# Value and key sums turned in one held-back transfer, and a unit's query sum turned by TensorE

## The chip, the cores and the metric

The kernel runs on one core of one Trainium2 chip. The metric is device time in microseconds (us) from one launch, the median over several runs. The engines of a core work in parallel, each on its own list of instructions in the order in which the program has them: TensorE (PE in the profile; its weight loads are PEld), VectorE (DVE), ScalarE (ACT), GpSimd (POOL) and SyncE (SP), which here does nothing but issue DMA transfers. An instruction that waits holds up everything behind it on its engine.

## The reference, cut to what matters

```python
def _A_ref(x, wqkv, wo):                       # x: 1 x 2048 x 576, 32 heads of 18
    q, k, v = split_heads(x @ wqkv)
    p = softmax(q @ k.T * 18 ** -0.5)
    return merge_heads(p @ v) @ wo

def _fwd_reference(...):
    g = sigmoid((x * gate_w).sum(-1, keepdims=True))
    return g * _A_ref(x, wqkv, wo) + (1 - g) * _B_ref(x, ...)

_out, _vjp = jax.vjp(_f, A_x, A_wqkv, A_wo, ...)
return (_out, *_vjp(grad_out))
```

The kernel returns the output and the gradients of all inputs. The attention part A takes the middle of the run. Its backward part needs, for every head, the gradients of q, k and v over all 2048 positions; they go to a DRAM tensor `dqkv_d`, from which later stages work out the gradients of x and wqkv. Part B, a long convolution, is worked on by GpSimd beside the attention and by all engines after it.

## The kernel before

The heads are taken in 8 groups of 4. A group's positions are cut into 4 blocks of 512, and one *unit* is one group with one block of queries: 32 units. A unit runs over 16 tiles of 128 keys, in 32 *steps* (the loop variable `G` counts steps over all units; the list of each engine is written out by hand in the order of the loop). The forward part of a unit runs 39 steps ahead of its backward part. Below, *s* counts the backward steps from the start of a group's last unit: 0 to 31 is that unit, and 32 to 63 is the first unit of the next group.

In each step TensorE makes scores in two layouts and the products with the gradient of the output (tiles `ps_P`). ScalarE takes two exponentials of them (`PT`, `eb`), VectorE two products (`ds`). The sums over them are collected in bursts, in slots that repeat every 8 steps: value sums (`accV`), query sums (`accQ`), a slot in which TensorE turns (transposes) something, key sums (`accK`), and another turn slot. With kq the block of 512 keys, the bursts of a unit end at steps 8 kq + 8 (values), 8 kq + 10 (queries) and 8 kq + 13 (keys).

The key sums need `ds` transposed. A tile of `ds` holds 4 heads by 512 queries. SyncE issues a transposing DMA for it (`dsT<-ds`, L1473) that turns 3 of the 4 heads for most tiles; the fourth is turned by TensorE in a turn slot, two tiles at a time (`turn`, L1105 on; `by_pe` says how many of a pair p of tiles TensorE turns: 2, but 0 for pair 5, which loses its slot to another job, and 1 for pair 6, which shares it). VectorE copies what TensorE turned out of PSUM. The two DMAs of pair p are issued in steps 4 p + 1 and 4 p + 3 of the unit, and the burst that needs them starts 6 steps after the second. There are 3 buffers for a pair.

The gradients come out with heads along partitions, and `dqkv_d` wants positions there, so each finished sum of 128 x 512 is turned as well (`store_grad`, L1080). Two steps after the burst's end SyncE issues a transposing DMA into a tile `gT` (3 buffers). Four steps later GpSimd copies the 18 useful columns of each head out of it into `dtk` (one buffer), and stores that by a DMA of its own. A query sum (`gb`) is ready at the end of every unit, and value and key sums (`dvacc`, `dkacc`, 4 buffers each, rounded to bfloat16 in place) at the end of every group: 32 + 32 + 32 of these transfers. In the steps s the value sums go at 10, 18, 26 and 34, the query sum at 36, and the key sums at 15, 23, 31 and 39.

SyncE's list holds, besides these, the loads of the next group's operands (`KaT`, `QaT`, `VaT`, and transposing `Ktok`, `Vtok`, `Qtok`) and the turn of part of `PT` (`PTt`, L1126). GpSimd's list holds the convolution's powers (`Eo`, `et`), which a budget deals out over the steps (`e_emit`; each pack of a gradient counts 1.4 us in it), and in step 2 of a forward unit two small products (`dOa`, `prod`, L1061 and L1063) for which VectorE waits one step later.

Of the kernel before, what the change touches and what calls it, by code (L numbers as in the profile page):

```python
# [11 lines left out]
BF = mybir.dt.bfloat16  # L12
# [5 lines left out]
P = 128  # L18


def build(tc, aps, dbg_aps=None, stages=("s1", "attn", "post", "s4", "final")):
    nc = tc.nc
# [16 lines left out]
    S, D = x2.shape  # L39
    H = 32  # L40
    DH = D // H
    F = 3 * D
    NT = S // P
    HP = 32
# [14 lines left out]
    NG = H // 4  # L59

    with ExitStack() as gctx:
# [20 lines left out]
        dqkv_d = dram.tile([P, NT, F], BF, name="dqkv_d")  # L82
# [497 lines left out]
        Q = {}  # L580
# [370 lines left out]
        if "attn" in stages:  # L951
            KB = 512
            NQ = S // KB
            TPQ = KB // P
# [4 lines left out]
            with ExitStack() as ctx:  # L959
# [67 lines left out]
                UN = {}  # L1027
                DKV = {}
# [47 lines left out]
                def in_place(t_):  # L1076

                    return t_.bitcast(BF)[:, 0:KB]

                def store_grad(gb, g, which, t0):  # L1080
                    c0 = which * D + g * 4 * DH
                    gT = work.tile([P, TPQ, 4, HP], BF, tag="gT", bufs=3, name="gT")
                    nc.sync.dma_start_transpose(out=gT.rearrange("p t a b -> p t (a b)"), in_=gb)

                    def pack():
                        dtk = work.tile([P, TPQ, 4, DH], BF, tag="dtk", bufs=1, name="dtk")
                        nc.gpsimd.tensor_copy(dtk, gT[:, :, :, 0:DH])
                        nc.gpsimd.dma_start(dqkv_d[:, t0:t0 + TPQ, c0:c0 + 4 * DH], dtk.rearrange("p t a b -> p t (a b)"))
                    packs.append((now[0] + 4, pack))

                packs, now = [], [0]

# [6 lines left out]

                def by_pe(u, p):  # L1100

                    return 2 if u == units[-1] else {NPF: 0, NPF + 1: 1}.get(p, 2)

                def turn(tiles, outs):

                    pt_ = apsp.tile([P, len(tiles), TPQ, P], BF, tag="accB", name="turn_p")
                    for x, t_ in enumerate(tiles):
                        for qb in range(TPQ):
                            nc.tensor.transpose(pt_[:, x, qb, :], t_[:, qb * P:(qb + 1) * P], ident_bf)  # L1109

                    def ev():
                        x = 0
                        for n, o_ in outs:
                            (nc.scalar.copy if NTOT <= now[0] < NTOT + OFF else nc.vector.tensor_copy)(o_(), pt_[:, x:x + n])  # L1114
                            x += n
# [12 lines left out]
                def turn_mid(i):  # L1128

                    U = UN[units[-1]]  # L1130
                    pt_ = s_pair("turn").rearrange("p a b -> p (a b)").bitcast(BF)[:, 0:2 * KB].rearrange("p (t b) -> p t b", b=P)
                    for x in range(2):
                        for qb in range(TPQ):
                            nc.tensor.transpose(pt_[:, x * TPQ + qb, :], U["ds"][i][:, 1 + x, qb * P:(qb + 1) * P], ident_bf)
                    d_ = U["dsT", i // 2][:, i % 2, TPQ:3 * TPQ, :]
                    return lambda: (nc.scalar.copy if now[0] < NTOT + OFF else nc.vector.tensor_copy)(d_, pt_)

                def do_tile(U):
                    U["dOaT"] = work.tile([P, TPQ, P], BF, tag="dOaT", name="dOaT")
# [10 lines left out]
                def at(n, f):  # L1150
                    todo.setdefault(n, []).append(f)
# [11 lines left out]
                def dv_half(g, b, kq, h, acc):  # L1163
                    U = UN[(g, b)]

                    def stored(ii):
                        for j in range(4):
                            w = KT if j < 2 else KB
                            mm(acc[HP * j:HP * (j + 1), 0:w], lhsT=U["dOa"][:, ii, j, :], rhs=U["eb"].pop((kq, ii, j)),
                               start=(ii == 0), stop=(ii == 3), tile_position=(0, HP * j))  # L1170

                    def turned(ii):
                        for j in range(2):
                            mm(acc[HP * j:HP * (j + 1), KT:KB], lhsT=U["dOa"][:, ii, j, :], rhs=U["PTt", kq][:, j * TPQ + ii, :],
                               start=False, stop=False, tile_position=(0, HP * j))
                    stored(2 * h)
                    turned(2 * h)
                    turned(2 * h + 1)
                    if h == 0:
                        stored(1)  # L1180
                    else:
                        late.append(lambda: stored(3))

                    def ev():
                        if b == 0:
                            DKV[("v", g, kq)] = work.tile([P, KB], F32, tag="dvacc", bufs=4, name="dvacc")
                            nc.vector.tensor_copy(DKV[("v", g, kq)], acc)
                            return
                        a_ = o_ = DKV[("v", g, kq)]
                        if b == NQ - 1:  # L1190
                            o_ = DKV[("v", g, kq)] = in_place(a_)
                        nc.vector.tensor_tensor(o_, a_, acc, op=A.add)  # L1192
                    return ev

# [18 lines left out]
                def dk_half(g, b, kq, h, acc):  # L1213
                    U = UN[(g, b)]
                    o_ = acc[:, 2 * h * P:2 * (h + 1) * P]
                    for qb in range(TPQ):
                        for j in range(4):
                            mm(o_[HP * j:HP * (j + 1), :].rearrange("p (a b) -> p a b", b=P), lhsT=grp_t[g]["Qtok", b][:, qb, HP * j:HP * (j + 1)],
                               rhs=U["dsT", 2 * kq + h][:, :, j * TPQ + qb, :], start=(qb == 0), stop=(qb == TPQ - 1), tile_position=(0, HP * j))

                    def ev():
                        if b == 0:
                            DKV[("k", g, kq)] = work.tile([P, KB], F32, tag="dkacc", bufs=4, name="dkacc")
                            nc.vector.tensor_copy(DKV[("k", g, kq)], acc)
                            return
                        a_ = o_ = DKV[("k", g, kq)]
                        if b == NQ - 1:
                            o_ = DKV[("k", g, kq)] = in_place(a_)
                        nc.vector.tensor_tensor(o_, a_, acc, op=A.add)
                    return ev  # L1230

# [110 lines left out]
                for G in range(NTOT + OFF + 24):  # L1342
# [37 lines left out]
                    if ("f1", G) in todo:  # L1380
                        acc = apsp.tile([P, KB], F32, tag="accO", name="accF")
                        evs.append(todo.pop(("f1", G))[0](acc))
                        e_done[0] += 1.4
                    elif G == NST + 5:
                        evs.append(turn(*do_tile(UN[units[0]])))
                    elif 0 <= m_ < NTOT // 8:
                        u_, kq = divmod(m_, NQ)
                        g, b = units[u_]
                        if slot in SLOTS:
                            nm, burst, h = SLOTS[slot]  # L1390
                            if h == 0:
                                acc = accB("acc" + nm)
                                fill(acc, NFILL[nm])
                                burst(g, b, kq, 0, acc)
                            else:
                                evs.append(burst(g, b, kq, 1, acc))
                                if nm == "Q" and kq == NQ - 1:
                                    at(("pre", G + 2), lambda g=g, b=b: store_grad(UN[(g, b)].pop("dqa"), g, 0, b * TPQ))
                                elif nm in "KV" and b == NQ - 1:
                                    at(("pre", G + 2), lambda g=g, kq=kq, nm=nm: store_grad(DKV.pop((nm.lower(), g, kq)), g, 1 + "KV".index(nm), kq * TPQ))  # L1400
# [541 lines left out]
```

## Time and profile before

| | us |
|---|---|
| median of 3 runs | 2599.77 |
| lowest and highest run | 2592.21, 2615.22 |
| the profiled execution, its own time | 2605.51 |
| its span from the first to the last instruction | 2603.5 |
| TensorE busy | 2263.8 (87%) |
| VectorE busy | 2279.8 (88%) |
| ScalarE busy | 2260.6 (87%) |
| GpSimd busy | 1838.9 (71%) |
| mean granted TensorE clock | 0.965 |

The page's sixth part lists the DMA issues by line: `dsT<-ds` 512 times, `PTt<-PT` 128 times, and `gT<-gb`, `gT<-dvacc` and `gT<-dkacc` 32 times each, all by SyncE as transposing transfers, and `dqkv_d<-dtk` 96 times by GpSimd. In the page's waits a line reads "engine line waited for: us in total, times, longest". In the table of windows each row is a stretch of time with the busy time of each engine, the number of its instructions, the granted TensorE clock (1.00 is full speed) and the mean busy share of the 16 DMA engines, which can be over 1 because packets overlap. In a timeline a row is the start, the time taken, the engine and line, and in brackets the idle time before it and what ended that. For SyncE the time taken is that of issuing, not that of the transfer.

### The profile page before, as it was taken

How to read it: one execution, taken by the hardware profiler on the slowest of the kernel's cores; microseconds unless marked ns; L12 is line 12 of the kernel's file. 1: busy time of each engine (PE TensorE's matmuls, PEld its weight loads, DVE VectorE, ACT ScalarE, POOL GpSimd, SP SyncE). 2: the span in 40 equal slices, each digit the busy share in tenths (PEclk: the TensorE clock that was granted, in tenths of full speed). 3: DMA queues.
4: the chain of work that ended last, by engine and by line, in shares of the span. 5: the costliest groups of instructions: out<-in, count | busy, mean ns of one | idle time of the engine just before them, and what ended most of it. 6: DMA issues, size and time to landing. Idle time of an engine off the chain costs nothing. (4 is left out here: it accounts for less than half of the span.)

```text
span 2603.5 us, 72402 instructions
## 1 busy us (share of the span) xinstructions
PE 2263.8 (87%) x28467; PEld 1163.1 (45%) x28467; DVE 2279.8 (88%) x4091; ACT 2260.6 (87%) x2760; POOL 1838.9 (71%) x2859
## 2 busy tenths in 40 slices
PE   7998888888888788788888888888889799999989
PEld 4433333333333333333333333333334699998656
DVE  4849898999899899889989998999997699999964
ACT  5579999999999999999999999999997599999211
POOL 0389988898889888979888988898951155555331
PEclk9979998999999999999989999999999799999999
DMA  7749999999999999999999999999989789997995
GB/s 236 198 119 184 170 191 194 193 189 198 189 192 188 198 200 179 196 195 183 187 203 178 188 194 203 182 191 199 175 170 180 199 240 264 267 261 238 276 251 133
DMA packets 1273708, 518.92 MB, mean 199 GB/s; under 512 B 1188513, under 2 KB 1226002, under 8 KB 1271062
## 3 DMA queue, kind: packets, MB, share of 16 engines
q1 hardware_dynamic: 1225446, 368.05, 74.8%
q0 software_dynamic: 45904, 140.73, 20.2%
q10 hardware_dynamic: 2016, 5.51, 0.7%
q8 instruction: 223, 3.65, 0.6%
q14 instruction: 119, 0.97, 0.1%
HBM read 149.42 MB, written 96.94 MB: 95 GB/s over the span
## 5 line engine op out<-in xcount | busy, mean ns | idle before, releaser
L1463 DVE TENSOR_TENSOR ds<-ps_P,PT 128x512 bf16<-128x512 f32 x2048 | 1321.8, 685 | 71.8 <-PE ps_P L30 61.2
L1453 ACT ACTIVATE PT<-ps_P 128x1024 bf16<-128x1024 f32 x1024 | 1111.3, 1086 | 18.9 <-PE ps_P L30 17.3
L1458 ACT ACTIVATE eb<-ps_P 128x896 bf16<-128x896 f32 x1024 | 995.6, 973 | 55.1 <-PE ps_P L30 54.4
L30 PE MATMUL ps_P<-dOaT,VaT_g 32*128 32x512 bf16 x2048 | 792.5, 390 | 7.1 <-DVE ds L1463 6.2
L30 PE MATMUL ps_P<-QaT_g,KaT_g 32*128 32x512 bf16 x2048 | 410.3, 390 | 198.7 <-ACT PT L1453 169.4
L507 POOL TENSOR_TENSOR et<-eG,eT 128x448 f32<-128x448 f32 x576 | 542.8, 963 | 10.8
L30 PE MATMUL ps_P<-KaT_g,QaT_g 32*128 32x384 bf16 (+1 forms) x2048 | 407.0, 365 | 4.4 <-ACT eb L1458 0.8
L30 PEld LDWEIGHTS <-KaT_g 32*128 32x128 bf16 x2048 | 161.0, 92 | 488.7 <-issue 464.6
L507 POOL TENSOR_TENSOR Eo<-et,et 128x448 bf16<-128x448 f32 x288 | 327.2, 1136 | 21.0
L30 PEld LDWEIGHTS <-QaT_g 32*128 32x128 bf16 x2048 | 107.0, 91 | 245.1 <-issue 209.1
L30 PE MATMUL accO<-PT,Vtok_g 128*32 128x512 bf16 x2048 | 215.4, 398 | 1.0 <-DVE Ob L1059 0.5
L30 PE MATMUL accV<-eb,dOa 128*32 128x384 bf16 (+1 forms) x2048 | 189.4, 375 | 8.1 <-DVE dsT L1114 7.3
L30 PE MATMUL accK<-dsT,Qtok_g 128*32 128x256 bf16 x4096 | 163.1, 280 | 31.0 <-DMA dsT<-ds 28.8
L30 PEld LDWEIGHTS <-VaT_g 32*128 32x128 bf16 x2048 | 184.3, 91 | 3.7 <-issue 2.1
L30 PE MATMUL accQ<-ds,Ktok_g 128*32 128x512 bf16 x2048 | 161.2, 392 | 23.6 <-DVE dvacc L1192 18.0
L1114 DVE COPY dsT<-turn_p 128x1024 bf16<-128x1024 bf16 (+1 forms) x216 | 139.7, 647 | 2.4 <-PE turn_p L1109 2.4
L1109 PE MATMUL turn_p<-ident_bf,ds 128*128 128x128 bf16 x1676 | 136.4, 224 | 2.0 <-DVE gb L1210 0.8
L30 PEld LDWEIGHTS <-dOa 128*32 128x32 bf16 x3072 | 79.4, 96 | 131.4 <-issue 96.4
L30 PEld LDWEIGHTS <-Qtok_g 128*32 128x32 bf16 x4096 | 88.1, 97 | 99.6 <-issue 79.2
L673 ACT COPY E1e<-etp 128x1024 bf16<-128x1024 bf16 x132 | 125.3, 1064 | 1.8 <-PE etp L672 1.8
L507 POOL TENSOR_TENSOR et<-eT 128x32 f32<-128x32 f32 (+3 forms) x288 | 116.3, 424 | 11.1
L1109 PEld LDWEIGHTS <-ds 128*128 128x128 bf16 x1676 | 99.2, 100 | 48.2 <-issue 48.0
(301 smaller groups left out, 3771.3 us busy)
## 6 DMA issues: line engine op xcount, KB each, us to landing
E_d<-Eo POOLq DMA_DIRECT2D x144, 256.0 KB, 3.6
E1n<-E_d POOLq DMA_DIRECT2D x30, 1024.0 KB, 6.9
T0w<-Kp_d SPq DMA_DIRECT2D x18, 1024.0 KB
xs<-xb_d POOLq DMA_DIRECT2D x28, 512.0 KB, 10.1
dsT<-ds SPq DMA_TRANSPOSE x512
dqkv_d<-dtk POOLq DMA_DIRECT2D x96, 72.0 KB, 4.5
Md_d<-mst SPq DMA_DIRECT2D x18, 288.0 KB
skw<-Md_d SPq DMA_DIRECT2D x72, 64.0 KB
```

What stands on the lines that cost most here:

```text
L30: return nc.tensor.matmul(out, lhsT=lhsT, rhs=rhs, start=start, stop=stop, **kw)
L507: nc.gpsimd.tensor_tensor(out, a, b, op=op)
L673: copy(E_[:, 4 * q:4 * q + 4], pt_)
L1109: nc.tensor.transpose(pt_[:, x, qb, :], t_[:, qb * P:(qb + 1) * P], ident_bf)
L1114: (nc.scalar.copy if NTOT <= now[0] < NTOT + OFF else nc.vector.tensor_copy)(o_(), pt_[:, x:x + n])
L1453: nc.scalar.activation(U["PT"][i, j // 2], ps, ACT.Exp)
L1458: nc.scalar.activation(e, ps.rearrange("p x q -> p (x q)")[:, KB - KT:2 * KB], ACT.Exp)
L1463: nc.vector.tensor_tensor(U["ds"][i][:, j, :], ps, U["PT"][i, j // 2][:, j % 2, :], op=A.mult)
```

## The change

- A group's value sum and key sum of the same block of keys are now put side by side in one buffer of `dvacc`: the key sum's last addition writes into its second half. One transposing DMA of twice the width turns both. It is issued 11, 19, 18 and 18 steps after the burst of the key sum for blocks 0 to 3 (2 steps in the last group), so at s = 24, 40, 47 and 55. GpSimd's two packs follow 4 and 6 steps later.
- A query sum is no longer turned by a DMA, but for the last two units. TensorE turns it in the next unit's slot of pair 1 (s = 43 at a group's end), together with one of the two tiles of that pair; VectorE copies it out of PSUM straight into `dtk`, and GpSimd only stores it, two steps later.
- For that, `by_pe` gives 1 for pair 1: the first tile of pair 1 is now turned whole (4 heads) by its DMA.
- `gT` has one buffer of double width in place of three, `dtk` has two in place of one.

```diff
-                def store_grad(gb, g, which, t0):
-                    gT = work.tile([P, TPQ, 4, HP], BF, tag="gT", bufs=3, name="gT")
+                def store_grad(gb, g, whichs, t0):
+                    n = len(whichs)
+                    gT = work.tile([P, 2 * TPQ, 4, HP], BF, tag="gT", bufs=1, name="gT")[:, 0:n * TPQ]
                     nc.sync.dma_start_transpose(out=gT.rearrange("p t a b -> p t (a b)"), in_=gb)
...
-                        dtk = work.tile([P, TPQ, 4, DH], BF, tag="dtk", bufs=1, name="dtk")
+                        dtk = work.tile([P, TPQ, 4, DH], BF, tag="dtk", bufs=2, name="dtk")
...
-                    packs.append((now[0] + 4, pack))
+                    for x in range(n):
+                        packs.append((now[0] + 4 + 2 * x, lambda x=x: pack(x)))
...
-                    return 2 if u == units[-1] else {NPF: 0, NPF + 1: 1}.get(p, 2)
+                    return 2 if u == units[-1] else {1: 1, NPF: 0, NPF + 1: 1}.get(p, 2)
...
+                def gb_tile():
+                    U, g, b = gq.pop(0)
+                    gb = U.pop("dqa")
+                    dtk = work.tile([P, TPQ, 4, DH], BF, tag="dtk", bufs=2, name="dtk")
+                    packs.append((now[0] + 2, lambda: nc.gpsimd.dma_start(dqkv_d[...], dtk.rearrange("p t a b -> p t (a b)"))))
+                    return [gb], [(0, lambda: dtk)]
...
+                            DKV.pop(("k", g, kq))
+                            o_ = DKV[("v", g, kq)].bitcast(BF)[:, KB:2 * KB]
...
-                                elif nm in "KV" and b == NQ - 1:
-                                    at(("pre", G + 2), lambda g=g, kq=kq, nm=nm: store_grad(...))
+                                elif nm == "K" and b == NQ - 1:
+                                    at(("pre", G + (2 if g == NG - 1 else (11, 19, 18, 18)[kq])), lambda g=g, kq=kq: store_grad(...))
...
+                            if p == 1 and gq:
+                                t2, o2 = gb_tile()
+                                t_, o_ = t2 + t_, o2 + o_
```

SyncE's list at the end of the third group, s = 31 to 39 before. The sizes are partitions, blocks of 128 and columns; a `dsT` of 12 blocks is 3 heads.

```order
L1083 DMA_TRANSPOSE gT_15843<-dkacc_12303 128x4x128
L1473 DMA_TRANSPOSE dsT_15798<-ds_15831 128x12x128
L1126 DMA_TRANSPOSE PTt_15915<-PT_14693 128x8x128
L1473 DMA_TRANSPOSE dsT_15943<-ds_15907 128x12x128
L1083 DMA_TRANSPOSE gT_15951<-dvacc_12416 128x4x128
L1473 DMA_TRANSPOSE dsT_15943<-ds_15973 128x12x128
L1019 DMA_TRANSPOSE Ktok_g_16014<-QKV_d_72 128x8x128
L1083 DMA_TRANSPOSE gT_16016<-gb_15975 128x4x128
L1473 DMA_TRANSPOSE dsT_16090<-ds_16051 128x12x128
L1009 DMA VaT_g_16104<-QKV_d_72 128x512
L1083 DMA_TRANSPOSE gT_16138<-dkacc_12599 128x4x128
L1473 DMA_TRANSPOSE dsT_16090<-ds_16127 128x12x128
```

SyncE's list after the change from the `Ktok` load on, s = 35 to 49.

```order
L1019 DMA_TRANSPOSE Ktok_g_15967<-QKV_d_72 128x8x128
L1495 DMA_TRANSPOSE dsT_16049<-ds_16002 128x16x128
L1009 DMA VaT_g_16058<-QKV_d_72 128x512
L1495 DMA_TRANSPOSE dsT_16049<-ds_16081 128x12x128
L1083 DMA_TRANSPOSE gT_16134<-dvacc_11777 128x8x128
L1130 DMA_TRANSPOSE PTt_16176<-PT_14940 128x8x128
L1495 DMA_TRANSPOSE dsT_16204<-ds_16164 128x12x128
L1009 DMA QaT_g_16239<-QKV_d_72 128x512
L1495 DMA_TRANSPOSE dsT_16204<-ds_16230 128x12x128
L1495 DMA_TRANSPOSE dsT_16349<-ds_16306 128x12x128
L1083 DMA_TRANSPOSE gT_16385<-dvacc_12077 128x8x128
L1495 DMA_TRANSPOSE dsT_16349<-ds_16376 128x12x128
```

The four single turns of s = 31 to 39 are gone, the first tile of pair 1 has 16 blocks, and the double turns of blocks 1 and 2 stand at s = 40 and 47; the second stands ahead of the second tile of pair 3.

GpSimd's list after the change at the same group's end, where the values of block 1, the query sum and the keys of block 1 are stored; `dtk_16247` is what VectorE wrote in step 43.

```order
L507 TENSOR_TENSOR et1_16271<-eG_1237,eT_1236 128x448
L1088 COPY dtk_16311<-gT_16134 128x288
L1089 DMA dqkv_d_75<-dtk_16311 128x4x72
L1149 DMA dqkv_d_75<-dtk_16247 128x4x72
L1088 COPY dtk_16382<-gT_16134 128x288
L1089 DMA dqkv_d_75<-dtk_16382 128x4x72
L507 TENSOR_TENSOR Eo_16132<-et0_16237,et1_16271 128x4x112
```

Before, nothing of the gradients stood here on GpSimd's list. With two `dtk` buffers in turn, the keys' copy takes the buffer that the query sum's store, right ahead of it, still reads; and the double turn at s = 47 takes the `gT` tile that this copy reads.

VectorE's list after the change in the slot of pair 1, where it has two copies; before there was one, of 128 x 2 x 512, for the two tiles of the pair.

```order
L1485 TENSOR_TENSOR ds_16230<-ps_P2_16245,PT_14825 128x512
L1118 COPY dtk_16247<-turn_p_16248 128x288
L1118 COPY dsT_16049<-turn_p_16248 128x512
L1485 TENSOR_TENSOR ds_16230<-ps_P2_16260,PT_14825 128x512
L1485 TENSOR_TENSOR ds_16306<-ps_P2_16276,PT_14865 128x512
```

The query sum's copy stands ahead of the tile's.

More of the change, by code (lines that the diff above doesn't have):

```diff
@@ L1113, in ev @@
                         for n, o_ in outs:
-                            (nc.scalar.copy if NTOT <= now[0] < NTOT + OFF else nc.vector.tensor_copy)(o_(), pt_[:, x:x + n])
-                            x += n
+                            src_ = pt_[:, x:x + n] if n else pt_[:, x].rearrange("p t (a b) -> p t a b", b=HP)[:, :, :, 0:DH]
+                            (nc.scalar.copy if NTOT <= now[0] < NTOT + OFF else nc.vector.tensor_copy)(o_(), src_)
+                            x += max(n, 1)
                     return ev
@@ L1190, in ev @@
                         if b == NQ - 1:
-                            o_ = DKV[("v", g, kq)] = in_place(a_)
+                            o_ = in_place(a_)
                         nc.vector.tensor_tensor(o_, a_, acc, op=A.add)
```

20 lines of the change are left out of this document (13 added, 7 removed).

## The prediction

> **What bounds the kernel now.** I read the waits of the attention stage first (235 to 1950 us), then a table of windows, then SyncE's timeline where a window was bad. Waits, in columns engine, line, waited for, total, times, longest:
>
> ```profile
> ACT eb L1458 <- PE ps_P L30: 44.3, 38, 4.6
> ...
> POOL dtk L1087 <- DMA dqkv_d<-dtk: 29.9, 19, 3.2
> ...
> PE accK L30 <- DMA dsT<-ds: 22.9, 13, 4.2
> ...
> DVE dOa L1069 <- POOL prod L1063: 7.3, 6, 2.1
> ```
>
> ScalarE hardly ever waits: 44.3 us here, in few long waits for TensorE, which in turn waits for the transposed `ds`. The windows say where. The first two rows and the first sum are of the 7 stretches at the ends of groups 1 to 7 (48 steps each), the last two are of the stretches between them.
>
> ```profile
> 822.00:912.00 90.00, 73.02 (x919) 29.40 (x916) 79.32 (x132) 83.99 (x98) 77.20 (x129) 0.96 1.10 198
> 1051.00:1144.00 93.00, 76.14 (x922) 30.11 (x921) 79.91 (x132) 84.90 (x98) 77.72 (x126) 0.93 1.05 198
> ...
> sum 623.00, PE 520.50 PEld 204.59 DVE 555.34 ACT 587.88 POOL 526.08; mean PE 74.36 PEld 29.23 DVE 79.33 ACT 83.98 POOL 75.15
> ...
> 683.00:822.00 139.00, 119.35 (x1511) 47.41 (x1508) 132.12 (x222) 138.92 (x161) 125.79 (x207) 1.00 1.03 187
> ...
> sum 1076.00, PE 920.69 PEld 363.55 DVE 1013.39 ACT 1065.85 POOL 946.29; mean PE 115.09 PEld 45.44 DVE 126.67 ACT 133.23 POOL 118.29
> ```
>
> Between the ends ScalarE is busy 138.92 of 139 us: it sets the pace there, 161 exponentials or 80 steps in 139 us, so **1.74 us a step**. At the ends it idles 623.0 - 587.9 = **35.1 us** in all, about 5 a group; between them 1076.0 - 1065.9 = 10.2 us. Only the 35.1 us stand near what the change moves. A third set of windows shows why a wait costs more than itself:
>
> ```profile
> 1340.00:1346.00 6.00, 4.97 (x59) 1.75 (x57) 5.62 (x11) 6.00 (x8) 3.84 (x9) 1.00 1.30 200
> ...
> 1349.00:1352.00 3.00, 0.90 (x16) 0.45 (x16) 0.00 (x0) 0.18 (x1) 1.15 (x4) 0.75 1.20 215
> 1352.00:1355.00 3.00, 3.00 (x27) 1.32 (x24) 2.21 (x4) 1.94 (x2) 2.83 (x8) 0.50 1.08 195
> ...
> 1361.00:1364.00 3.00, 3.00 (x26) 0.46 (x18) 1.92 (x3) 2.34 (x3) 2.63 (x4) 0.50 1.03 197
> ```
>
> After a wait of some 3 us the clock is at 0.50 for 12 us, TensorE is busy throughout and ScalarE starves: between 0.7 and 1.1 us lost in each 3 us, so about 3 us behind a wait of 3. A wait under a microsecond has no such tail to show.
>
> The cause, in SyncE's timeline at the end of group 3 (start, time to issue), with TensorE's wait last:
>
> ```profile
> 878.85 1.38 SPq L1019 DMA_TRANSPOSE Ktok_g<-QKV_d  x1
> 880.32 1.61 SPq L1083 DMA_TRANSPOSE gT<-gb  x1
> 882.02 1.67 SPq L1473 DMA_TRANSPOSE dsT<-ds  x1
> 883.74 0.57 SPq L1009 DMA_DIRECT2D VaT_g<-QKV_d  x1
> 884.42 1.20 SPq L1083 DMA_TRANSPOSE gT<-dkacc  x1
> 885.70 1.44 SPq L1473 DMA_TRANSPOSE dsT<-ds  x1
> 887.25 1.63 SPq L1126 DMA_TRANSPOSE PTt<-PT  x1
> ...
> 891.40 1.05 PE L30 MATMUL accK<-dsT,Qtok_g 128*32 128x256 bf16 x16 [3.36 <-DMA dsT<-ds]
> ```
>
> SyncE issues without a gap. It is late: VectorE finished this query sum from 869.42 on, and its turn goes out 10.9 us later; in the first unit of all the same two stand 3.9 us apart.
>
> ```profile
> 869.42 0.68 DVE L1210 SCALAR_TENSOR_TENSOR gb<-accQ,dqa 128x512 bf16<-128x512 f32 x1
> ...
> L1210 DVE SCALAR_TENSOR_TENSOR gb<-accQ,dqa x32: 680/681/692, 239.7 to 2018.6; 128x512 bf16<-128x512 f32 x32
> ...
> 243.62 1.19 SPq L1083 DMA_TRANSPOSE gT<-gb  x1
> ```
>
> So SyncE is about 7 us behind, and the tile issued at 885.70 was wanted at 888.0 (891.40 less the wait of 3.36) and came at 891.4. Its flight, issue included, was 5.7 us.
>
> **The change, part by part.** *Single turns go from the crowded place.* Each costs SyncE 1.2 to 1.25 us:
>
> ```profile
> L1083 SPq DMA_TRANSPOSE gT<-dvacc x32: 1194/1246/2259, 369.3 to 2026.6; - x32
> L1083 SPq DMA_TRANSPOSE gT<-dkacc x32: 1191/1195/2352, 376.6 to 2032.2; - x32
> ```
>
> Between s = 10 and 39, nine of them (8 and the query's) make 9 x 1.23 = 11 us; one double turn at s = 24 comes in, at about 1.3 us, what the equally wide `PTt` takes in the tail rows below. SyncE gains 9.8 us over these 30 steps of 52 us and was 7 behind at their end, so the backlog should be gone at s = 39, and with it the waits of pair 1. The most this can bring is the 35.1 us. The bytes stay: every query sum that a DMA no longer turns is replaced by a fourth head of `ds` in pair 1, two tiles' time earlier than its need.
>
> *Double turn at s = 47, with one `gT` buffer.* It waits until GpSimd has copied the keys of block 1, and SyncE holds everything behind it. No row shows this wait; it is built from these (the last is the landing of GpSimd's stores of `dtk`):
>
> ```profile
> 1288.36 1.27 SPq L1083 DMA_TRANSPOSE gT<-dvacc  x1
> ...
> 1298.58 0.43 POOL L1087 COPY dtk<-gT 128x288 bf16<-128x288 bf16 x1
> 1299.31 0.80 POOL L1088 DMA_DIRECT2D dqkv_d<-dtk  x1 [0.29 <-POOL dtk L1087]
> ...
> DMA to landing us min/median/max: 2.5/4.5/7.9
> ```
>
> From a turn's issue to GpSimd's copy, four steps later on the list, it is 10.2 us, of which GpSimd's own lateness is about 1.5. So after an issue at step 40 the values' copy starts at 10.2 us, the query's store 1.5 later (0.43 + 0.29 + 0.80), and the keys' copy must await its landing, 4.5 us: 16.2, done at 16.6. Step 47 starts at 7 x 1.74 = 12.2 us. SyncE is held 4.5 to 5.4 us (the second if the turn at 40 is as late as the 0.9 us in this row). The tile behind it, the second of pair 3, then goes at 5 + 1.3, lands 4.6 (a wait in group 2, below) to 6.2 us later, at 10.9 to 12.5 us; the burst that needs it starts 6 steps on, at about 10.4 + 0.6 = 11.0. A wait of 0 to 1.5 us, too short for the slow clock: I take 1 us a group, **7 us**. The ends: nothing, if GpSimd runs early; up to 10 us a group (a rival, below). At s = 55 GpSimd has two more steps of which one is lost to its lateness; a hold of 1 to 2 us there is inside pair 5's slack.
>
> ```profile
> 626.89 2.46 SPq L1473 DMA_TRANSPOSE dsT<-ds  x1
> ...
> 631.46 1.04 PE L30 MATMUL accK<-dsT,Qtok_g 128*32 128x256 bf16 x16 [1.65 <-DMA dsT<-ds]
> ```
>
> *VectorE.* One copy of 1024 columns becomes one of 512 and one of 288:
>
> ```profile
> L1114 DVE COPY dsT<-turn_p 128x1024 bf16<-128x1024 bf16 x186 | 127.1, 683 | 2.4 <-PE turn_p L1109 2.4
> ...
> L1114 DVE COPY dsT<-turn_p 128x512 bf16<-128x512 bf16 x30 | 12.6, 419 | 0.0
> ...
> L1059 DVE TENSOR_TENSOR Ob<-accF,rl 128x288 bf16<-128x288 f32 x32 | 14.6, 457 | 1.1
> ```
>
> By the line through the first two, 288 columns take 155 + 288 x 0.52 = 303 ns: 39 ns more, 30 times, **1.2 us**; with 457 ns as upper end 5.8 us; nothing as lower end, since VectorE has 7 us to spare in the 139 us above. *TensorE* turns 8 blocks in that slot as before: nothing. *GpSimd* loses 30 copies of 0.43 us and most waits for its one `dtk` buffer (29.9 us above), and gains the 3.7 us wait a group just built. It is not the bound, but when it is late VectorE waits (`dOa <- prod`, 7.3 us above), and the 10.2 us between the ends hang on that. I cost it at nothing, between -6 and +8 us. *The end of attention*: SyncE has three singles fewer ahead of the last double turn (3.7 us), which lands later by its second half, and GpSimd's two copies after it hold `pidx_i`, for which ScalarE waited:
>
> ```profile
> 2009.08 1.26 SPq L1126 DMA_TRANSPOSE PTt<-PT  x1
> ...
> 2024.24 1.19 SPq L1083 DMA_TRANSPOSE gT<-dkacc  x1
> ...
> 2029.49 0.43 POOL L1087 COPY dtk<-gT 128x288 bf16<-128x288 bf16 x1 [5.53 <-DMA gT<-dkacc]
> ...
> ACT RX L604 <- DVE l1col L1506: 16.6, 1, 16.6
> ```
>
> I take **-1 us**, between -4 and +3.
>
> **The sum**, against the profiled execution's own 2605.5 us (span 2603.5, 2 us around it): -35.1 + 7 + 1.2 + 0 - 1 = -28, so 2577.5. That execution is 5.7 us above the median of the runs, 2599.8, and from that the same sum gives 2572. How much of the 5.7 is such waits is not shown; I put 2574.
>
> **The rivals.** *The same bytes (no change).* If the waits come from the load on the DMA engines and not from the number of issues, merging helps little: the share of the DMA engines is 1.10 and 1.05 in the bad windows, but also 1.03 in a clean one, and 1.30 in one with ScalarE fully busy. For it speaks that issues stretch there (2.46 us above for a usual 1.4) and that the `Ktok` and `VaT` loads stay. Half of the 35.1 would remain: -17.5 + 7 + 0.2 = -10, 2590, up to 2600. The Trainium skill, in "DMA: Bandwidth & Descriptors", section "Issuing engines are not separate DMA queues", says that all transfers run on the same 16 engines and that the time to initiate one is usually small relative to it; by that page the merging itself would be worth little and this rival's 2590 to 2600 would be the forecast. Here the issue is 1.44 of 5.7 us and SyncE has no gap, so the trace does not bear it out at the groups' ends.
>
> *SyncE held too long (slower).* The hold at s = 47 is 5 us by a median landing. With the longest, 7.9 us, and GpSimd 3 us later from its own wait, it is 11 to 12, the tile lands at 17 to 19.5 us, TensorE waits 6 to 8 and the slow clock adds 3: 10 us, 7 times, 70, so 2600 - 35 + 70 = 2635. It decides from a hold of about 8 to 9 us, where wait and tail give back the 5 us a group.
>
> *All of it goes (faster).* No hold matters, and GpSimd's shorter list clears the 10.2 us as well: 2600 - 35 - 10 + 1 = 2556.
>
> **Chances.** Forecast, 2564 to 2583: 0.48. All goes: 0.16. Same bytes: 0.24. Held: 0.12. About 1%, 26 us, is what a measurement can tell from no change, so the line is at 2574. Above it in speed lie "all goes" and three fifths of the forecast: 0.16 + 0.30 = 0.46. Slower by over 1% is most of "held": 0.09. Within: 0.45. The range 2552 to 2600 leaves out "held" and a little below.
>
> **What would show it.** Right: no `accK` wait for `dsT` at pair 1 after a group's end, ScalarE's idle at the 7 ends under 12 us, the clock there at 1.00, 34 turns into `gT`. The hold shows as a SyncE wait for GpSimd's `dtk` at s = 47, about 5 us, 7 times, and a small `accK` wait 6 steps on. Wrong would be: `accK` waits of 3 us left at the old place (same bytes), or new ones at pair 3 with the clock at 0.50 (held), or `dOa <- prod` waits that grow past 15 us.

## The result, and the profile after

| | median, us | lowest to highest | runs |
|---|---|---|---|
| before | 2593.68 | 2589.88 to 2615.22 | 6 |
| the change | 2569.56 | 2566.3 to 2575.52 | 6 |

The medians differ by 24 us. The ratio, over all the runs, is 0.9894, with a 95% interval of 0.9867 to 0.9921. A second measurement later, beside other runs of the kernel before, gave 0.9899 (0.9884 to 0.9914). The profiled execution took 2574.3 us (span 2572.5), 31 us less than that of before.

The waits of the attention stage after the change (235 to 1925 us; before, where the stage ends 30 us later, to 1950), in total, times and longest:

```profile
ACT eb L1480 <- PE ps_P L30: 21.2, 19, 3.7
...
PE accK L30 <- DMA dsT<-ds: 11.9, 8, 3.3
...
DVE dOa L1069 <- POOL prod L1063: 2.6, 4, 0.9
```

ScalarE's waits are halved (44.3 before), TensorE's for `ds` as well (22.9), and VectorE's for `prod` fell from 7.3. The windows show where. Two rows and the sum of the 7 groups' ends, cut at the same steps as before (97 or 98 exponentials each):

```profile
588.00:676.00 88.00, 73.83 (x919) 29.51 (x919) 79.50 (x134) 84.36 (x98) 74.78 (x120) 0.96 1.12 206
815.00:898.00 83.00, 70.33 (x906) 28.31 (x906) 78.46 (x132) 82.87 (x97) 70.64 (x118) 1.00 1.06 194
...
sum 591.00, PE 500.24 PEld 200.95 DVE 551.69 ACT 583.64 POOL 507.19; mean PE 71.46 PEld 28.71 DVE 78.81 ACT 83.38 POOL 72.46
```

And two rows and the sum of the stretches between them, from 239 us to the last exponential as before:

```profile
445.00:588.00 143.00, 122.14 (x1497) 47.46 (x1495) 131.98 (x224) 138.46 (x160) 125.18 (x206) 0.96 1.02 190
...
898.00:1042.00 144.00, 121.03 (x1521) 48.28 (x1519) 132.81 (x225) 139.63 (x162) 126.96 (x208) 0.99 1.04 193
...
sum 1078.00, PE 921.09 PEld 364.48 DVE 1014.26 ACT 1066.30 POOL 952.43; mean PE 115.14 PEld 45.56 DVE 126.78 ACT 133.29 POOL 119.05
```

ScalarE idles 591.0 - 583.6 = 7.4 us at the ends (35.1 before) and 1078.0 - 1066.3 = 11.7 us between (10.2). Together the two kinds of stretches took 1699 us and now take 1669: 26 of these 30 us are ScalarE's idle time (45.3 to 19.1), and 4 are a little less busy time of the same exponentials.

The 11.7 us are not the idle time that was there before. In the two rows above ScalarE idles 4.5 and 4.4 us, behind two new waits of TensorE at 456 and 910 us (shown below). They come from the turns of a group's end and lie just past the stretches counted as ends. Of the 10.2 us of before, 8.7 were in three stretches, of which these are two:

```profile
239.00:365.00 126.00, 107.50 (x1328) 42.02 (x1321) 115.99 (x194) 122.23 (x142) 111.41 (x170) 0.96 0.95 179
1597.00:1740.00 143.00, 122.07 (x1511) 47.42 (x1510) 132.62 (x223) 139.46 (x161) 129.09 (x221) 0.98 0.98 185
```

In each of the three VectorE had waited for GpSimd's `prod` (1.52 us at 287 us, 1.28 at 1209, 2.12 at 1608). After the change the same three stretches have 1.9 us of idle time left. So of the 26 us about 19 lie at the groups' ends, where the prediction looked for the gain (35.1 less 7.4 and 8.9), and about 7 where GpSimd had been late.

What idle time is left at the ends has a new place, and the 0.96 of the row from 588 us comes from there. TensorE's timeline at that group's end, with the wait in brackets:

```profile
668.93 1.04 PE L30 MATMUL accK<-dsT,Qtok_g 128*32 128x256 bf16 x16 [2.51 <-DMA dsT<-ds]
```

SyncE's timeline ahead of it (x2 are two issues in one row):

```profile
653.95 5.78 SPq L1495 DMA_TRANSPOSE dsT<-ds  x2
662.21 1.23 SPq L1083 DMA_TRANSPOSE gT<-dvacc  x1
663.54 1.50 SPq L1495 DMA_TRANSPOSE dsT<-ds  x1
```

And windows of 3 us around the wait, with the granted clock third from the end:

```profile
666.00:669.00 3.00, 0.46 (x7) 0.25 (x10) 1.04 (x2) 1.71 (x2) 2.54 (x5) 0.85 1.27 162
669.00:672.00 3.00, 3.00 (x31) 1.21 (x31) 1.55 (x3) 1.27 (x2) 2.52 (x8) 0.50 1.13 293
672.00:675.00 3.00, 3.00 (x27) 1.06 (x25) 2.31 (x4) 2.46 (x3) 2.54 (x7) 0.51 1.10 197
675.00:678.00 3.00, 2.57 (x35) 0.96 (x32) 2.47 (x4) 2.95 (x5) 2.78 (x7) 1.00 1.20 260
```

This is the hold at s = 47. The double turn goes out at 662.21, and the second tile of pair 3 only behind it, at 663.54; the burst of pair 3 (s = 53) waits 2.51 us for that tile, and the clock is at 0.50 for 6 us. Why the turn was held stands in GpSimd's timeline:

```profile
655.45 0.81 POOL L1089 DMA_DIRECT2D dqkv_d<-dtk  x1 [0.30 <-POOL dtk L1088]
656.28 0.98 POOL L507 TENSOR_TENSOR et<-eG,eT 128x448 f32<-128x448 f32 x1
657.18 0.79 POOL L1149 DMA_DIRECT2D dqkv_d<-dtk  x1
661.77 0.42 POOL L1088 COPY dtk<-gT 128x288 bf16<-128x288 bf16 x1 [3.79 <-DMA dqkv_d<-dtk]
```

The keys' copy waits 3.79 us for the landing of the query sum's store (line 1149) right ahead of it, since that holds the buffer of `dtk` that the copy needs. Over the stage SyncE waits in this way 24.2 us, 6 times (SyncE's own waits):

```profile
SPq L1083 <- POOL dtk L1088: 24.2, 6, 5.2
```

Of the `accK` waits over 1.2 us two are at pair 3 (the other is of 1.40 us, at 1344 us) and two at pair 5, s = 61, behind the turn at s = 55: one of 2.48 us at 456 us, and the one in the last line here, TensorE's. The first two lines are SyncE's, the turn at s = 55 and the tile behind it:

```profile
903.50 1.27 SPq L1083 DMA_TRANSPOSE gT<-dvacc  x1
904.82 3.32 SPq L1495 DMA_TRANSPOSE dsT<-ds  x1
...
910.28 0.92 PE L30 MATMUL accK<-dsT,Qtok_g 128*32 128x256 bf16 x16 [3.27 <-DMA dsT<-ds]
```

Here the turn is not held: in none of the seven groups does SyncE wait for GpSimd at s = 55. SyncE is late there by long issues: 4.05 us for a load and 4.53 for two tiles ahead of the turn, and 3.32 for the tile itself (4.27 in the other case), where the median of all 512 tiles is 1.60. Why these issues stretch was not followed.

### The profile page after: what moved, and what is told of

The parts are those of the page before. It is cut to its first block, busy times and chain, and to the rows that moved or that the text cites. A ratio compares the mean times of both kernels' runs of the same rounds, so it can differ in the third digit from the quotient of the medians.

```text
span 2572.5 us, 72343 instructions
## 1 busy us (share of the span) xinstructions
PE 2246.0 (87%) x28463; PEld 1164.1 (45%) x28463; DVE 2277.3 (89%) x4121; ACT 2257.6 (88%) x2760; POOL 1825.5 (71%) x2829
## 5 line engine op out<-in xcount | busy, mean ns | idle before, releaser
L30 PE MATMUL ps_P<-QaT_g,KaT_g 32*128 32x512 bf16 x2048 | 404.5, 385 | 202.5 <-ACT PT L1475 172.5
L30 PE MATMUL accV<-eb,dOa 128*32 128x384 bf16 (+1 forms) x2048 | 184.0, 366 | 9.3 <-DVE dsT L1118 8.5
L1118 DVE COPY dsT<-turn_p 128x1024 bf16<-128x1024 bf16 (+1 forms) x216 | 130.9, 606 | 1.2 <-PE turn_p L1112 1.2
L1112 PE MATMUL turn_p<-ident_bf,ds 128*128 128x128 bf16 x1552 | 126.6, 222 | 1.7 <-DVE gb L1226 1.0
L560 POOL DMA_DIRECT2D E_d<-Eo x144 | 85.1, 591 | 42.8 <-POOL Eo L507 42.8
```

The costliest lines, as they stand in the source:

```text
L30: return nc.tensor.matmul(out, lhsT=lhsT, rhs=rhs, start=start, stop=stop, **kw)
L560: nc.gpsimd.dma_start(E_d[:, q // EQ, 0:EQ * 2 * P], Eo.pop(q).rearrange("p c r n -> p (c r n)"))
```

## The experiments

All ratios are to the kernel before, run on the same chip as the kernels sent with it.

| kernel | value and key turns | query sum turned by | `dtk` buffers | ratio, 95% interval |
|---|---|---|---|---|
| query only | single, as before | TensorE | 2 | 0.9999 (0.9979 to 1.002) |
| singles held | single, held back | TensorE | 2 | 0.9964 (0.9947 to 0.9981) |
| pairs at once | double, 2 steps after the keys | TensorE | 2 | 0.9912 (0.9883 to 0.994) |
| pairs only | double, held | SyncE | 1 | 1.0017 (0.9999 to 1.0035) |
| pairs only, later | double, held one step longer | SyncE | 1 | 1.0037 (1.0018 to 1.0057) |
| own buffers | double, held one step longer | TensorE | 1 + 1 | 0.9985 (0.9963 to 1.0007) |
| pairs, two buffers | double, held one step longer | SyncE | 2 | 0.987 (0.9853 to 0.9887) |
| the change again | double, held | TensorE | 2 | 0.9899 (0.9884 to 0.9914) |
| early store | double, held | TensorE | 2 | 0.9873 (0.9838 to 0.9907) |
| one later | double, held one step longer | TensorE | 2 | 0.9901 (0.9866 to 0.9935) |
| both | double, held one step longer | TensorE | 2 | 0.9862 (0.983 to 0.9894) |
| both again | the same kernel | TensorE | 2 | 0.9865 (0.9845 to 0.9886) |

"One step longer" is for the turns of blocks 2 and 3, s = 48 and 56; in "pairs, two buffers" that of block 1 goes one step later too, at s = 41. The waits below are of one profiled execution of each kernel, from 235 to 1925 us. Such an execution can lie off its kernel's median: it took 9 us more for "pairs at once", 7 more for "own buffers", 10 more for "pairs, two buffers" and 12 less for "both again".

**Which part earns it: the query's move alone.** Value and key sums stay single turns as before, with `gT` of single width in two buffers.

```diff
-gT = work.tile([P, 2 * TPQ, 4, HP], BF, tag="gT", bufs=1, name="gT")[:, 0:n * TPQ]
+gT = work.tile([P, TPQ, 4, HP], BF, tag="gT", bufs=2, name="gT")
...
-elif nm == "K" and b == NQ - 1:
-    at(("pre", G + (2 if g == NG - 1 else (11, 19, 18, 18)[kq])), lambda g=g, kq=kq: store_grad(..., (2, 1), kq * TPQ))
+elif nm in "KV" and b == NQ - 1:
+    at(("pre", G + 2), lambda g=g, kq=kq, nm=nm: store_grad(..., (1 + "KV".index(nm),), kq * TPQ))
```

> The query sum is turned by TensorE as in the change, but value and key sums go as single turns at their old steps (s = 10 to 39). Backlog theory (what counts is how many issues stand in SyncE's list at a group's end): only one of nine issues is gone, so the waits for dsT at pair 1 after a group's end stay for the most part, ScalarE idles 20 to 30 us at the seven ends, and the time is 0 to 10 us under the kernel before. Query theory (the query sum's turn, right ahead of pair 1's tiles, was what made them late): those waits go, under 10 us of idle at the ends, and the time is within 5 us of the changed kernel's 2570 or better, since nothing is held.

2593.75 us, 0.9999. The old waits are all there:

```profile
ACT eb L1479 <- PE ps_P L30: 32.7, 26, 6.2
PE accK L30 <- DMA dsT<-ds: 25.0, 15, 5.8
```

GpSimd has no copies of query sums left, SyncE one turn less a unit, and TensorE's waits for `ds` are no shorter (22.9 before): the query's turn alone was not what made SyncE late. The kernel has the second `dtk` buffer too, so that the buffer and the query's move together bring nothing with single turns.

**The double turns alone.** The query sum goes by SyncE again, into a buffer of its own, and `dtk` has one buffer as before.

```diff
-gT = work.tile([P, 2 * TPQ, 4, HP], BF, tag="gT", bufs=1, name="gT")[:, 0:n * TPQ]
+gT = (work.tile([P, 2 * TPQ, 4, HP], BF, tag="gT", bufs=1, name="gT") if n == 2 else
+      work.tile([P, TPQ, 4, HP], BF, tag="gTq", bufs=1, name="gTq"))
...
-dtk = work.tile([P, TPQ, 4, DH], BF, tag="dtk", bufs=2, name="dtk")
+dtk = work.tile([P, TPQ, 4, DH], BF, tag="dtk", bufs=1, name="dtk")
...
-return 2 if u == units[-1] else {1: 1, NPF: 0, NPF + 1: 1}.get(p, 2)
+return 2 if u == units[-1] else {NPF: 0, NPF + 1: 1}.get(p, 2)
...
-if nm == "Q" and kq == NQ - 1 and u_ < NU - 2:
+if nm == "Q" and kq == NQ - 1 and False:
```

> Value and key sums go as held-back double turns as in the change, but each unit's query sum keeps its single turn by DMA at s = 36 (a buffer of its own), and pair 1 keeps two tiles on TensorE. Backlog theory: eight of nine issues are gone from s = 10 to 39, so the old waits at pair 1 are gone (under 5 us of idle from them), and the time is 2565 to 2580; the keys' copy no longer waits for the query's store, so the hold at s = 47 shrinks from 3.5 us to 1 to 2 us. Query theory: the wait at pair 1 stays at half or more, 2580 to 2592.

2602.91 us, 1.0017, above what either theory allowed. GpSimd waits longer than before for its one `dtk` buffer (29.9 before, 19 times), and so does SyncE for GpSimd (36.9 us, 11 times):

```profile
POOL dtk L1088 <- DMA dqkv_d<-dtk: 42.0, 24, 4.7
ACT eb L1480 <- PE ps_P L30: 38.4, 27, 6.2
PE accK L30 <- DMA dsT<-ds: 20.2, 8, 5.9
DVE dOa L1069 <- POOL prod L1063: 10.6, 6, 5.3
```

The same kernel with the turns of blocks 2 and 3 one step later:

```diff
-(11, 19, 18, 18)[kq]
+(11, 19, 19, 19)[kq]
```

> As the run with pairs alone (query sums keep their single turn by DMA and GpSimd's copy), with the double turns of blocks 2 and 3 one step later, so that the hold, which was longer there, does not stand ahead of pairs 3 and 5. If the hold alone ate that run's gain: the 20 us of accK waits there fall under 6 and the time is 2568 to 2578, so the query's move to TensorE is worth 10 us or less. If the query's turn and copy are what matters: 2585 or more.

2606.53 us, 1.0037. The `accK` waits fell to 11.0 us and nothing was won: VectorE's waits for `prod` rose to 36.3 us. So with double turns GpSimd became late. From these two runs I took it that the query sum had to leave GpSimd and SyncE too; two later runs show that this was wrong.

**Merging or holding back.** Two single turns at the times of the double one:

```diff
-store_grad(DKV.pop(("v", g, kq)).bitcast(BF), g, (2, 1), kq * TPQ)
+t_ = DKV.pop(("v", g, kq)).bitcast(BF)
+store_grad(t_[:, 0:KB], g, (2,), kq * TPQ)
+store_grad(t_[:, KB:2 * KB], g, (1,), kq * TPQ, 2)
```

> As the change, but each double turn is issued as two single turns, one behind the other, at the same held-back steps (two gT buffers of single width). Backlog theory (the place counts, not the merging): the old waits are gone all the same; the four more issues of 1.2 us stand in the next unit, two of them right ahead of the second tiles of pairs 3 and 5, so the new waits there are the same or up to 5 us more in all: 2568 to 2582. Merging theory (fewer transfers is what helps): half of the gain or more is lost, 2582 to 2594.

2586.8 us, 0.9964: a third of the gain, as the merging theory has it. Added up from the trace, the `accK` waits at pair 1 of a group's first unit fall from 11.9 us to 1.4, but at pair 5, where two issues now stand ahead of the second tile, they rise to 10.1; they are 17.5 us in all. And the double turn without holding, 2 steps after the key sum:

```diff
-(2 if g == NG - 1 else (11, 19, 18, 18)[kq])
+2
```

> As the change, but the double turns are not held back: they go two steps after the key sum's burst (s = 15, 23, 31, 39). Backlog theory: between s = 10 and 39 four issues of 1.3 us stand where nine of 1.23 us stood, half of the backlog goes, waits at pair 1 stay at 5 to 15 us in all, none at pairs 3 and 5 of the next unit: 2570 to 2582. Merging theory: all old waits go and there is no hold in the next unit, so it is faster than the change, 2552 to 2564.

2570.93 us, 0.9912: most of the gain, though `accK` waits of 17.2 us stay.

```profile
ACT eb L1480 <- PE ps_P L30: 28.8, 27, 4.1
POOL dtk L1088 <- DMA dqkv_d<-dtk: 17.3, 7, 4.9
PE accK L30 <- DMA dsT<-ds: 17.2, 10, 3.7
```

Merging at the held times is worth 0.9964 - 0.9894 = 0.7% (18 us), and the intervals lie apart; holding back a merged turn 0.9912 - 0.9894 = 0.2%, which is within them. Without holding, merging is worth 0.9999 - 0.9912 = 0.9%, from "query only" to this kernel, and these intervals lie apart as well. The bytes are the same in all of these; what merging changes on SyncE is the number of issues. That the issues are the reason is argued from this: a fixed cost that a transfer has elsewhere than on SyncE would show the same. Nor is the whole gain seen at the old place: added up from the traces, the `accK` waits at pair 1 of a group's first unit are 17.4 us in "query only", 12.9 in this kernel and 11.9 before.

**What the hold costs.** First the query sum's store at s = 43 in place of 45, so that it has landed when the keys' copy wants the buffer:

```diff
-packs.append((now[0] + 2, lambda: nc.gpsimd.dma_start(dqkv_d[...], ...)))
+packs.append((now[0] + 0, lambda: nc.gpsimd.dma_start(dqkv_d[...], ...)))
```

> One edit against the change: GpSimd stores a query sum in the step in which TensorE turns it (s = 43) and not two steps later, so that the keys' copy at s = 46 finds its dtk buffer free. Hold theory (the waits at pairs 3 and 5 of the next unit come from SyncE being held for the one gT buffer): GpSimd's seven waits for the landing of a store (20 us in the change) go, SyncE's wait for dtk falls from 24.7 to under 10 us, the waits at pair 3 (4.3 us) go, those at pair 5 may stay: 3 to 8 us faster than the change, 2561 to 2567. Load theory (the double turn's bytes make the tiles late, held or not): same as the change, 2567 to 2573.

2564.5 us, 0.9873, which the interval does not tell from the change. GpSimd's waits for `dtk` fell from 20.0 to 8.0 us, SyncE's for GpSimd from 24.2 to 15.3 (under 10 was expected). The waits at pair 5 stayed (6.2 us, 5.8 in the change). Then the turns of blocks 2 and 3 one step later, which gives GpSimd more time and puts the turn behind the second tile of its pair (the edit shown above, on the change):

> One edit against the change: the double turns of blocks 2 and 3 go one step later (s = 48 and 56), behind the second tiles of pairs 3 and 5 in SyncE's list and not ahead of them. Hold theory: those tiles no longer stand behind the wait or the double turn, the waits at pairs 3 and 5 go (10 us of waits and their slow clock, some 15 us of ScalarE's idle time), 2553 to 2562; the hold itself shrinks by one step. Load theory: the same bytes at nearly the same time, waits of the same size move to pairs 4 and 6 or stay: 2566 to 2574.

2569.61 us, 0.9901, no faster than the change. The `accK` waits nearly go (3.2 us), but the `prod` waits rise to 8.1 us: GpSimd's copies too now come a step later, nearer to `prod`. Both edits together:

> Both edits of the two runs before: early store and one step later. Hold theory: no SyncE wait for dtk over 1 us and no accK wait at pairs 3 and 5; what is left are GpSimd's late products and the tail: 2550 to 2560, faster than either edit alone by no more than 5 us. Load theory: 2566 to 2574.

2561.34 us, 0.9862. To see whether that beats the change, the two were run on one chip:

> The change as it stands, on the same chip as the next kernel, so that the two can be set side by side. Theory (the waits at pairs 3 and 5 of the next unit that the held SyncE and the double turn at s=55 leave are worth 5 to 10 us): ratio to the kernel before 0.988 to 0.991, and the next kernel 0.2 to 0.4% under it. Rival (these waits are made good by later slack): the two kernels within 0.1% of each other.

> The change with the query's store two steps earlier (s=43) and the third and fourth turn's triggers moved one step later. Theory: ratio 0.985 to 0.988, 5 to 10 us under the change, with matmul waits for the ds transfer of 4 to 8 us against some 12 in the change. Rival: the same ratio as the change within 0.1%, the waits moved but not the time.

2570.6 us (0.9899) and 2563.44 us (0.9865): 7.2 us apart, and the intervals (0.9884 to 0.9914, 0.9845 to 0.9886) touch only at their ends. The waits of the second:

```profile
ACT eb L1480 <- PE ps_P L30: 14.7, 21, 1.8
POOL dtk L1088 <- DMA dqkv_d<-dtk: 7.4, 4, 2.9
DVE dOa L1069 <- POOL prod L1063: 3.2, 4, 1.1
...
PE accK L30 <- DMA dsT<-ds: 1.6, 2, 1.0
```

**One shared pair of buffers, or one each.** The kernel of the last run, with the same number of `dtk` buffers, but one for the packs and one for the query sums:

```diff
 def pack(x):
-    dtk = work.tile([P, TPQ, 4, DH], BF, tag="dtk", bufs=2, name="dtk")
+    dtk = work.tile([P, TPQ, 4, DH], BF, tag="dtk", bufs=1, name="dtk")
...
 def gb_tile():
-    dtk = work.tile([P, TPQ, 4, DH], BF, tag="dtk", bufs=2, name="dtk")
+    dtk = work.tile([P, TPQ, 4, DH], BF, tag="dtq", bufs=1, name="dtk")
```

> The previous kernel, but with one buffer of dtk for the packed value and key sums and one of its own for the query sums, in place of two that all three share. It tells apart why the double turns without the query's move lost. Theory that the single buffer makes GpSimd late: GpSimd waits over 35 us in all for dtk's store, VectorE waits over 15 us for prod, time 2575 to 2595. Theory that it was the query's copy on GpSimd and its turn on SyncE: prod waits under 8 us, time 2560 to 2570 although GpSimd waits for the buffer.

2594.94 us, 0.9985: nearly the whole gain is gone by this alone, 31 us. Both ways from a late GpSimd to the other engines show: VectorE waits 27.0 us for `prod` (3.2 in the kernel of the last run), and SyncE 29.2 us for GpSimd's copies (5.2), with `accK` waits of 12.6 us (1.6).

```profile
POOL dtk L1088 <- DMA dqkv_d<-dtk: 53.1, 26, 5.9
ACT eb L1480 <- PE ps_P L30: 42.8, 32, 4.8
DVE dOa L1069 <- POOL prod L1063: 27.0, 8, 7.6
PE accK L30 <- DMA dsT<-ds: 12.6, 6, 3.8
```

Seven of the eight `prod` waits are at s = 60, one at each group's end; `prod` itself stands at s = 59 in GpSimd's list. GpSimd's timeline there, with the two packs of block 2 (s = 52 and 54) ahead of `prod`, and VectorE's wait:

```profile
907.60 0.76 POOL L1089 DMA_DIRECT2D dqkv_d<-dtk  x1 [0.29 <-POOL dtk L1088]
...
913.62 0.42 POOL L1088 COPY dtk<-gT 128x288 bf16<-128x288 bf16 x1 [3.91 <-DMA dqkv_d<-dtk]
...
919.07 0.69 POOL L1063 TENSOR_TENSOR prod<-dOa,Ob 128x288 f32<-128x288 bf16 x1
```

```profile
919.80 0.46 DVE L1069 TENSOR_REDUCE dOa<-prod 128x16 bf16<-128x288 f32 x1 [7.57 <-POOL prod L1063]
```

The two packs of a double turn stand two steps (3.5 us) apart, and a store's landing takes 4.4 us by the median (page of the change, DMA issues); with one buffer the second copy must wait for it, here 3.91 us. All 26 waits are of second copies (of 28), and `prod` stands a few instructions behind the packs of block 2 in each group. How the rest of the 7.57 us is made up was not followed.

**Two buffers, but the query sum by SyncE.** If the buffer is what the double turns lacked in the two "pairs only" kernels, then they should pay with it, and without any move of the query sum. It is turned into the shared `gT`, and GpSimd copies it 3 steps later (4 before); the turn of block 1 goes one step later to leave room for it.

```diff
-packs.append((now[0] + 4 + 2 * x, lambda x=x: pack(x)))
+packs.append((now[0] + (4 if n == 2 else 3) + 2 * x, lambda x=x: pack(x)))
...
-return 2 if u == units[-1] else {1: 1, NPF: 0, NPF + 1: 1}.get(p, 2)
+return 2 if u == units[-1] else {NPF: 0, NPF + 1: 1}.get(p, 2)
...
-if nm == "Q" and kq == NQ - 1 and u_ < NU - 2:
+if nm == "Q" and kq == NQ - 1 and False:
...
-(11, 19, 18, 18)[kq]
+(11, 20, 19, 19)[kq]
```

> The value and key sums in double turns at s=24, 41, 48 and 56, two dtk buffers as in the change, but the query sums turned by SyncE's transfer (into the same gT buffer, s=36) and copied by GpSimd, as before. It is the kernel with double turns alone that lost (1.0017, and 1.0037 one step later), with the one thing added that it had lacked: the second dtk buffer. Theory (the second buffer is what the double turns need; the query's move is worth little): GpSimd's waits for dtk's store under 25 us, VectorE's waits for prod under 8 us, ratio 0.985 to 0.992. Rival (the query has to leave SyncE and GpSimd too): prod waits over 10 us or SyncE's waits for dtk over 30 us, ratio 0.995 to 1.003.

2566.25 us, 0.987 (0.9853 to 0.9887): as much as the best kernel that moves the query sum.

```profile
ACT eb L1480 <- PE ps_P L30: 22.5, 24, 3.0
POOL dtk L1088 <- DMA gT<-gb: 10.4, 6, 3.5
PE accK L30 <- DMA dsT<-ds: 9.4, 7, 2.4
DVE dOa L1069 <- POOL prod L1063: 3.9, 4, 1.8
```

GpSimd's waits for a store's landing are gone from the list. So the part of the change that does not show in its description decides: two buffers of `dtk` that the two packs of a double turn take in turn. With them the query's move to TensorE is worth nothing that these runs can tell (0.987 against 0.9865); with one buffer for the packs it was worth 0.5% (1.0037 to 0.9985), the query's own buffer included. The kernel differs from the "pairs only" ones in the few steps named above too; that the buffer is the cause rests on the run with one buffer each, which changes nothing else that reaches the packs.

## Why the prediction was right, and where it was not

The forecast was 2574 us, and 2569.56 came. From the profiled execution the sum said -28 us, and the two profiled executions differ by 31.2. The medians differ by 24.1, from a median before that came out 6 us lower over six runs than over the three of the prediction. Part of how close the forecast came is luck: two terms that it put at nothing, GpSimd and the waits at pair 5, came out at about -7 and +9 us.

- *The waits behind the late query and key turns go (-35.1).* Right in place and cause. No `accK` wait over 1 us is left at pair 1, and one of 1.0 us at s = 37; 34 turns into `gT` are left, and a double one takes SyncE hardly longer than a single one from the same tile did (1270 against 1246 ns):

```profile
L1083 SPq DMA_TRANSPOSE gT<-dvacc x32: 1232/1270/2855, 391.9 to 2000.2; - x32
L1083 SPq DMA_TRANSPOSE gT<-gb x2: 1196/1229/1262, 1930.0 to 1996.5; - x2
```

- *The hold at s = 47 (+7).* The hold itself came as built: 4.5 to 5.4 us a group was forecast, and SyncE waited 24.2 us in 6 of the 7 groups, 4.0 each and at most 5.2. What it costs did not. "A wait of 0 to 1.5 us, too short for the slow clock" failed: of four waits at pair 3 two were under 0.5 us, but that of 1.40 us at 1344 us has 9 us at 0.50 behind it, as the one of 2.51 us has its 6:

```profile
1344.00:1347.00 3.00, 2.76 (x28) 0.98 (x28) 1.29 (x2) 1.08 (x3) 2.41 (x4) 0.50 1.42 237
1347.00:1350.00 3.00, 3.00 (x29) 1.38 (x28) 2.58 (x4) 2.46 (x3) 2.69 (x5) 0.50 0.86 186
1350.00:1353.00 3.00, 2.96 (x25) 0.63 (x21) 1.59 (x3) 2.88 (x4) 2.82 (x4) 0.50 1.17 258
```

  "A hold of 1 to 2 us there is inside pair 5's slack" failed too: no hold came at s = 55, and yet two waits of 2.48 and 3.27 us came at pair 5, costed at nothing. In the profiled execution ScalarE idles at most 7.4 us behind the waits at pair 3 (all of the ends) and 8.9 behind those at pair 5, 16 us for a term of 7. The two kernels on one chip, of which the second has hardly any of these waits, differ by 7.2 us in the median. So the places did not hold, and whether the size did is not settled. New waits at pair 3 with the clock at 0.50, which the prediction had named as a sign of being wrong, came at two group ends and did not make the kernel slower.
- *VectorE (+1.2).* The copy was put at 303 ns by the line through two widths and measured 298:

```profile
L1118 DVE COPY dtk<-turn_p x30: 298/298/299, 255.4 to 1886.7; 128x288 bf16<-128x288 bf16 x30
```

- *GpSimd (nothing, between -6 and +8).* Its waits went as said: those of before are gone, and the 20.0 us that are left are seven waits for the query sum's store, one a group, 2.9 us each where 3.7 was forecast. The term was not nothing, though: the `prod` waits fell by 4.7 us, and ScalarE's idle time where GpSimd had been late fell by about 7. What the second buffer carries was not seen. The double turns bring packs 3.5 us apart, and without that buffer these make waits that cost 31 us, more than the whole gain. The prediction set these packs against a landing for the hold alone.
- *The end of attention (-1).* The span behind the last exponential is 2603.5 - 1937.9 = 665.6 us before and 2572.5 - 1908.4 = 664.1 after: -1.5. The last exponential `PT` starts at 1937.9 and 1908.4 us. In the profile of the change run again the same span is 2566.7 - 1903.4 = 663.3 us, so that a term of 1 us is hardly above the scatter.

The prediction's reading of the slow clock was a little off as well. Of the four windows behind the wait at 1351 us ScalarE loses 0.4 to 1.1 us in each (2.7 in all), not 0.7 to 1.1; the sum of about 3 us stands.

Of the rivals, *the same bytes* fell. With the bytes the same, two single turns at the double one's times give 0.9964 and the double one 0.9894. The Trainium skill says in "DMA: Bandwidth & Descriptors", section "Issuing engines are not separate DMA queues", that the time to initiate a transfer is usually small relative to it; here merging alone was worth 0.7%, so that rule does not decide this case. *SyncE held too long* did not come: the longest hold was 5.2 us, under the 8 to 9 from which it would decide. *All of it goes* (2556) did not come either; the kernel with both edits, at 2561 and 2563, is near it, and it needed the query's store two steps earlier and two turns one step later. The description named two moves. The prediction read the turns rightly; the query's move it counted among the nine singles that leave the crowded place, and the runs show no gain from it, neither beside single turns nor beside double ones with two buffers.

## What to carry to other kernels

On an engine that issues transfers without a gap, count the transfers and not only the bytes: one transfer of twice the width cost its issuer what one single cost, and merging was worth 18 us here, while holding the merged one back was worth too little to tell. Before merging, ask who empties the merged transfer: two stores that now follow each other closer than a store's landing (3.5 against 4.4 us) need two buffers, and a buffer that is too few makes an engine late that seemed off the path. A part of a change is tested with the buffers of the whole: the double turns without the second buffer seemed to need the query's move, and did not.

## What the runs showed of the hardware

A wait of TensorE has no fixed tail of slow clock, and the longer wait does not have the longer tail. Before the change the clock was at 0.50 for 12 us behind a wait of 3.20 us (at 1351 us, the prediction's windows) and for 6 behind one of 3.36 us (at 891 us). After it the clock was at 0.50 for 9 us behind 1.40 us and for 6 behind 2.51 us (both above), and behind the 3.27 us at 910 us for about 3:

```profile
910.00:913.00 3.00, 2.72 (x29) 0.99 (x29) 1.33 (x3) 1.05 (x2) 2.60 (x4) 0.58 1.07 184
913.00:916.00 3.00, 2.36 (x29) 1.19 (x27) 2.82 (x6) 2.63 (x4) 2.66 (x5) 0.86 1.16 248
```

The prediction's "A wait under a microsecond has no such tail to show" does not hold either: before the change a wait of 0.95 us (at 432 us) has three such windows behind it, 433 to 442 us, and those of 0.76 and 0.35 us at 1018 and 1577 us have none. The price of a wait is therefore good only as a mean over several of them. What decides the length of the tail was not followed.
